# A ring of ten half-size units, one transfer for each piece, in a cached-attention decode step

## The chip, the cores and the metric

The kernel runs on one core of one Trainium2 chip. The metric is the device time of that core in microseconds (us), lower is better; a kernel's time is the median over its runs. The profile describes one execution, and its span runs from the first to the last instruction.

## What is computed

One decode step mixes an attention block over a long cache with a small gated MLP, for four sequences of one token each:

```python
x = A_x                                            # [4, 1, 1024], bf16
g = sigmoid((x * gate_w).sum(-1, keepdims=True))
# attention block: H = 32 heads of 128, Sk = 8192 cached keys
q = (x @ wq) split into heads
scores = einsum("bhqd,bhkd->bhqk", q, k_cache) * 128 ** -0.5
o = einsum("bhqk,bhkd->bhqd", softmax(scores), v_cache)
a = merge_heads(o) @ wo
# MLP block: with one token per sequence the routing always selects it
y = (silu(x @ w_gate) * (x @ w_up)) @ w_down * sigmoid(x @ w_r)
b = x + y
out = g * a + (1 - g) * b
```

`k_cache` and `v_cache` are [4, 32, 8192, 128] in bf16, 268 MB each. The weights together are some 39 MB. Each byte is read once.

## The kernel before, in words

**Pieces.** K and V are each read in ND = 32 pieces. A piece is four heads of one sequence: 128 partitions (four heads by 32 stretches of 256 keys), 64 KB on each, 8.4 MB in all. K piece d and V piece d belong to the same heads. Eight pieces make a group g (GD = 8), which has one softmax. A piece has RD = 4 quarters of 64 keys per partition, 16 KB each, numbered n.

**Order.** The program is one sequence, and PE, DVE and POOL run it in exactly that order. It starts with the query weights (wq), the gate weights, K0, K1 and the up weights; then K2 to K7; then K8, V0, K9, V1 and so on, V running eight pieces behind K. After K31 come the down weights (`wd_piece`) and V23 to V31. The output weights wo come last, in blocks of 1 MB and less. All loads are issued by SP in this order; a load waits on SP until the part of the ring that it overwrites has been read, and the loads after it wait behind it.

**The ring.** All of these loads land in one SBUF buffer of 160 KB per partition. Before, it has NS = 5 slots of 32 KB, half a piece each. `slots(2)` deals them out by turns, so successive pieces take slots 0-1, 2-3, 4-0, 1-2, 3-4 and again. A piece on two adjoining slots is one transfer; one on slots 4 and 0 is two transfers of 4 MB. Pieces V26 to V28 are always in two halves (`apart`), and V29 to V31 are cut further.

**A K piece** (`k_pair`). DVE transposes eight half-quarters (steps 0 to 7, two for each quarter) from the ring into one of three buffers TB (L494); for each step PE multiplies it with the spread query Z, eight matmuls into the scores S_ps (L499). So the ring is read by DVE alone here, and quarter n has been read when step 2n+1 is done. The quarters are used in the order 0 to 3.

**A V piece** (`v_pair`). PE alone reads the ring: 64 matmuls, 16 for each quarter, into the sums o_ps (L579), weighted by PB, the spread probabilities.

**Work hung onto the steps of K pieces.** After every second V piece the sums are emptied: ACT writes the first part (L605), and three DVE operations (L609, `sums`) add the others into OS. They are queued in `full` and flushed after step 2 of the next K piece. `finish`, eight small matmuls and in some pieces a sum more (L625), is flushed after step 4, and the scaling into OT (L637, `late`) after step 6. For the first group, softmax is put into the steps of K8: its `first` part after step 0 (maxima, then the exponential on ACT into a TB buffer, L530) and its `second` part after step 1 (transpose into PT, L535, then the spreading into PB on ACT and POOL). For the later groups both run right behind the last K piece of the group.

**The change of stage after K31.** The PSUM banks of the scores are given up (`scores.close()`) and taken over by the accumulator `acc` of the output. So `wd_piece`, whose matmuls (L287) write `acc`, comes on PE behind K31 and behind the exponential that reads the last scores. It reads the down weights row block by row block: 27 rows of 2 KB per partition with two matmuls each, then five shorter ones, in that order. V23 comes on PE behind it.

Of the kernel before, what the change touches and what calls it, by code (L numbers as in the profile page):

```python
# [8 lines left out]
BF = mybir.dt.bfloat16  # L9
# [103 lines left out]
def kernel(  # L113
# [15 lines left out]
    nc = tc.nc  # L129
    P = 128  # L130
# [20 lines left out]
    NB = 512  # L151
    NH = D // NB
    RING = JR * Dh
    NS = 5
    assert Sq == 1 and Dh == P and D % P == 0 and F % (P * FR) == 0
    assert H % GH == 0 and JR == 128 and RD * GD == QP and D % NB == 0
    scale = float(Dh) ** -0.5
# [11 lines left out]
    nc.at_finalize(drop_implied)  # L169
    nc.at_finalize(begin_early)  # L170

    ring = const.tile([P, NS, RING], BF, name="ring")
    turn = [0]


# [5 lines left out]
        tb_turn[0] += 1  # L181
        return t[0:rows, 0:n] if dtype == BF else t[0:rows, 0:2 * n].bitcast(dtype)

    def slots(n):
        at = turn[0]
        turn[0] = (at + n) % NS
        return at

    flat = ring[:].rearrange("p s n -> p (s n)")

    def load_pair(src, n, apart=False):

        a = slots(2)
        if a + 1 < NS and not apart:
            lo = a * RING
            nc.sync.dma_start(out=flat[:, lo:lo + 2 * n], in_=src)
            return [flat[:, lo:lo + n], flat[:, lo + n:lo + 2 * n]]
        halves = [ring[:, a], ring[:, (a + 1) % NS]]
        for i, half in enumerate(halves):
            nc.sync.dma_start(out=half[:, 0:n], in_=src[:, i * n:(i + 1) * n])  # L200
        return halves


    S0 = scp.tile([P, 4, NB], F32, name="S_ps")
# [8 lines left out]
        return b[:, 0:n].rearrange("p (%s) -> p %s" % (" ".join(names), " ".join(names)), **dict(zip(names, shape)))  # L213

    N = H * Dh
    wq_at = load_pair(A_wq.rearrange("(c t) n -> c (t n)", t=DT), DT // 2 * N)
    NX = Bn + 2
    x6 = const.tile([NX, D], BF)
    nc.sync.dma_start(out=x6[0:Bn], in_=x2)
# [134 lines left out]

    def gu_piece(view, w_i):

        ws = load_pair(view.rearrange("(c t) f -> c (t f)", t=DT), TW * F)

        def cols(w, t, i):
            row = w[:, t * F:t * F + FB].rearrange("p (f m) -> p f m", m=FI)  # L360
            if i < FG - 1:
                return [(0, FR, row[:, :, FR * i:FR * i + FR])]
            return [(0, FR - 1, row[:, :, FR * i:FI]), (FR - 1, FR, w[:, t * F + FB:(t + 1) * F])]
        x_rows(o_ps[w_i], ws, FG, cols)
# [28 lines left out]
        nc.vector.tensor_tensor(out=hS[:], in0=hs_ps[0:72], in1=cS[:], op=ALU.mult)  # L393

    def wd_piece():
        a = slots(2)
        assert a + 1 < NS and (FI + SX) * D == 2 * RING
        w = flat[:, a * RING:(a + 2) * RING]
        at = FI * D
        nc.sync.dma_start(out=w[:, 0:at], in_=wdv)  # L400
        for u in range(2):
            nc.sync.dma_start(out=w[32 * u:32 * u + 12, at:at + SX * D], in_=wd_apart[u])
        nc.sync.dma_start(out=w[64:72, at:at + D], in_=wd_rest)
        parts = [(hT[:, i // FR, i % FR, :], w[:, i * D:(i + 1) * D]) for i in range(FI)]
        parts += [(hS[:, v, :], w[0:72, at + v * D:at + (v + 1) * D]) for v in range(SX)]
        for i, (lhsT, rows) in enumerate(parts):
            for n in range(NH):
                mm_acc(n, lhsT, rows[:, n * NB:(n + 1) * NB], start=(i == 0))
# [11 lines left out]
                                 rhs=OT[:, WB * g0 + k:WB * g1:WB, :], start=True, stop=True, skip_group_check=True)  # L420
        nc.vector.tensor_copy(out=LT[:, :, g0:g1, :], in_=lp)  # L421

    wo_home = {}

    def wo_block(g, r0=0, r1=FR, half=None):

        home, at = divmod(g, 4)
        if home not in wo_home:
            wo_home[home] = ring[:, slots(1)].rearrange("p (g r n) -> p g r n", g=4, r=FR)
        w = wo_home[home][:, at]  # L430
        if half is None:
            nc.sync.dma_start(out=w[:, r0:r1].rearrange("p r n -> p (r n)"),
                              in_=wov[:, g, r0:r1].rearrange("p r n -> p (r n)"))
        else:
            nc.sync.dma_start(out=w[:, r0, half * NB:(half + 1) * NB], in_=wov[:, g, r0, half * NB:(half + 1) * NB])

        def use():
            for r in range(r0, r1):
                for n in range(NH) if half is None else [half]:
                    mm_acc(n, LT[:, r, g, :], w[:, r, n * NB:(n + 1) * NB])  # L440
        return use
# [25 lines left out]
    def kv_view(cache, d):  # L467
        b, h0 = heads(d)
        return cache[b, h0:h0 + NQ].rearrange("h (r j) d -> (h r) (j d)", j=2 * JR)
# [8 lines left out]
    def k_pair(d):  # L478
        g, t = divmod(d, GD)
        Z = Zt[d % 2]  # L480
        if d == 0:
            spread(0)
        if t == 0:
            S_ps[g] = S0
        sps = S_ps[g]
        ks = load_pair(kv_view(A_k_cache, d), RING)
        for n in range(RD):
            kn = ks[n // JT].rearrange("p (c j h m) -> p c h j m", c=JT, h=2, m=Dh // 2)[:, n % JT]
            s = QP - 1 - (RD * t + n)
            for half in range(2):  # L490
                step = 2 * n + half
                flat_t = turned(P, CJ * Dh // 2)
                T = flat_t.rearrange("p (j i e) -> p j i e", j=CJ, e=2)
                nc.vector.transpose(out=flat_t.bitcast(U32).rearrange("p (j i) -> p j i", j=CJ), in_=kn[:, half].bitcast(U32))  # L494
                if step < 2 and ahead:
                    ahead.pop(0)()
                for e in range(2):
                    for z in range(4):
                        nc.tensor.matmul(sps[:, z, :], lhsT=Z[:, 2 * half + e, s:s + P], rhs=T[:, 16 * z:16 * z + 16, :, e],  # L499
                                         start=(t + n + half + e == 0),  # L500
                                         stop=(t == GD - 1 and n == RD - 1 and half + e == 2))
                if step == 2:
                    flush_sums()
                if step == RD and d + 1 < ND:
                    spread(d + 1)
                if step == RD:
                    flush()
                if step == RD + 2:
                    flush_late()
        if t == GD - 1:  # L510
            ahead.extend(softmax(g))
            while g > 0 and ahead:
                ahead.pop(0)()

    def softmax(g):
        sps = S_ps.pop(g)
        PTs = turned(P, 4 * NB)

        def first():

            nc.vector.tensor_reduce(out=mx[:, 0:1], in_=sps[:].rearrange("p z n -> p (z n)"), axis=AX.X, op=ALU.max)  # L521
            nc.vector.transpose(out=mxT[:].bitcast(U32), in_=mx[:].bitcast(U32))
            gm = stat.tile([P, GD], F32, tag="gm")
            nc.vector.tensor_reduce(out=gm[:], in_=mxT[:].rearrange("p (t r) -> p t r", r=RD), axis=AX.X, op=ALU.max)
            nc.vector.tensor_scalar(out=ng[:].rearrange("p (t r) -> p t r", r=RD), in0=gm[:].unsqueeze(2).to_broadcast([P, GD, RD]),
                                    scalar1=-scale, scalar2=None, op0=ALU.mult)
            nc.vector.transpose(out=ngT[:].bitcast(U32), in_=ng[:].bitcast(U32))  # L527
            negm = ngT
            rs = stat.tile([P, 1], F32, tag="rs")
            nc.scalar.activation(out=PTs, in_=sps[:].rearrange("p z n -> p (z n)"), func=ACT.Exp, bias=negm[:, 0:1], scale=scale, accum_out=rs[:, 0:1])  # L530
            rs_t[g] = rs

        def second():
            PT = ptp.tile([P, CJ, 32], BF, name="PT", tag="PT")
            nc.vector.transpose(out=PT[:].rearrange("p j i -> p (j i)"), in_=PTs)  # L535
            PT_t[g] = PT
            if g == 0:
                spread_p(0, NW)
            elif g == NG - 1:
                spread_p(GD * g, NW - 1)  # L540

        return [first, second]
# [16 lines left out]
    def v_pair(d):  # L559
# [4 lines left out]
        flush_sums()  # L564
        vv = kv_view(A_v_cache, d)
        if d < ND - 3:
            vs = load_pair(vv, RING, apart=d >= ND - GD + 2)
        else:
            vs = [ring[:, slots(1)] for _ in range(2)]
            for half, cuts in ((0, 1), (1, 2)) if d < ND - 1 else ((0, 2), (1, 4)):  # L570
                for c in range(cuts):
                    lo, hi = c * RING // cuts, (c + 1) * RING // cuts
                    nc.sync.dma_start(out=vs[half][:, lo:hi], in_=vv[:, half * RING + lo:half * RING + hi])
        for u in range(4 * RD):
            n, z = divmod(u, 4)
            vn = vs[n // JT]
            for w in range(4):
                j0 = CJ * (n % JT) + 16 * z + 4 * w
                nc.tensor.matmul(o_ps[w // 2][row:row + NM, w % 2, :],  # L579
                                 lhsT=PB[:, RD * (d % NW) + n, z].rearrange("p w s j -> p (w s j)"),  # L580
                                 rhs=vn[:, j0 * Dh:(j0 + 4) * Dh], start=(u == 0), stop=(u == 4 * RD - 1),
                                 skip_group_check=True)
            if u == 1:
                flush()
            if u == 7:
                flush_late()
# [132 lines left out]
```

## Time and profile before

The runs took 1342.68 to 1342.78 us, median 1342.69.

| what | value |
|---|---|
| span of the profiled execution | 1340.5 us |
| PE, DVE, ACT, POOL busy | 1067.9, 638.3, 57.7, 66.6 us |
| bytes read | 575.68 MB, 429 GB/s over the span |
| granted TensorE clock, mean | 0.912 of full |
| one transpose of a K step (L494) | 2278 ns, 256 of them |
| one V sum on DVE (L609) | 737 ns, 33 of them |
| wq, the first transfer, issue to landing | 21.9 us |

The profile has the busy time of each engine, the span in 40 equal slices (a digit is the busy share in tenths), the chain of work that ended last, groups of equal instructions with what ended the idle time before them, and the transfers by source line. A timeline gives start, length and the releaser of single instructions. The trace also has each packet that a DMA engine moved, and for each transfer the times at which the 16 DMA engines reported their shares as landed; a transfer counts as landed with the last of the 16.

### The profile page before, as it was taken

Reading aid. Unit: us, or ns where it says so; the run is one execution under the profiler, and the core shown is the slowest. Engines: PE = TensorE matmul, PEld = TensorE weight load, DVE = VectorE, ACT = ScalarE, POOL = GpSimd, SP = SyncE. Lnnn points to the kernel's source line nnn. Section 1 sums busy time; section 2 is a strip of 40 time slices with the busy share of each in tenths; the row PEclk is TensorE's granted clock in tenths of the full one; section 3 lists DMA queues with packets and bytes.
Section 4 is the critical chain, followed back from the end, with each engine's and each line's share of the span. In section 5 each row is a group of like instructions: output and inputs, shape, how many; then the busy total and the mean of one; then the engine's idle time right before and its main releaser. Section 6 shows DMA issues by size and latency. Waiting matters only on the chain.

```text
span 1340.5 us, 6937 instructions
## 1 busy us (share of the span) xinstructions
PE 1067.9 (80%) x4654; PEld 141.3 (11%) x1422; DVE 638.3 (48%) x385; ACT 57.7 (4%) x58; POOL 66.6 (5%) x174
## 2 busy tenths in 40 slices
PE   2666878887778788777879778789697879889888
PEld 0101000001011010101001010101011011111111
DVE  2555988556544347554436256646145555100001
ACT  0000000100010000100010000100000000110000
POOL 2000000100010000100010000100001000100000
PEclk9787999898998998898989888899898889889889
DMA  9999999999999999999999999999999999999998
GB/s 415 433 436 435 437 436 424 438 430 430 435 437 426 439 431 428 433 438 431 434 433 433 436 433 438 419 434 431 438 433 441 426 423 435 438 425 430 429 425 348
DMA packets 15512, 576.14 MB, mean 430 GB/s; under 512 B 1740, under 2 KB 2004, under 8 KB 3170
## 3 DMA queue, kind: packets, MB, share of 16 engines
q1 hardware_dynamic: 15474, 575.69, 99.7%
q8 instruction: 24, 0.39, 0.1%
q14 instruction: 6, 0.05, 0.0%
q10 hardware_dynamic: 8, 0.00, 0.0%
HBM read 575.68 MB, written 0.01 MB: 429 GB/s over the span
## 4 chain that ended last, share of the span: by engine, by line
DMA 62%; DVE 22%; PE 13%; another core or an unknown queue 1%; issue 0%; ACT 0%; SPq 0%; DVEq 0%
DMA ring<-in_A_k_cache_dram 51%; DVE TB L494 20%; DMA ring<-in_A_v_cache_dram 9%; PE o_ps L579 8%; PE S_ps L499 2%; PE acc L287 2%; DVE OS L609 2%; DMA x<-in_gate_w_dram 2%; DVE mx L521 0%; PE o_ps L333 0%; PE S_ps L333 0%; PE led L625 0%; DVE PT L535 0%; ACT TB L530 0%
## 5 line engine op out<-in xcount | busy, mean ns | idle before, releaser
L494 DVE STREAM_TRANSPOSE TB<-ring 128x2048 uint32<-128x2048 uint32 x256 | 568.2, 2278 | 471.7 <-DMA ring<-in_A_k_cache_dram 463.9
L499 PE MATMUL S_ps<-TB,Z 128*128 128x512 bf16 x2048 | 531.5, 414 | 186.0 <-DVE TB L494 178.4
L579 PE MATMUL o_ps<-ring,PB 128*64 128x512 bf16 x2048 | 468.5, 392 | 44.9 <-DMA ring<-in_A_v_cache_dram 43.7
L499 PEld LDWEIGHTS <-Z 128*128 128x128 bf16 x512 | 53.0, 103 | 649.6 <-issue 649.6
L579 PEld LDWEIGHTS <-PB 128*64 128x64 bf16 x512 | 57.6, 112 | 447.8 <-issue 443.4
L617 DVE SCALAR_TENSOR_TENSOR OS<-o_ps,mE,OS 128x512 f32<-128x512 f32 x5 | 3.8, 751 | 134.9 <-ACT OS L615 134.9
L476 POOL COPY Z<-qa 32x4 bf16<-32x4 bf16 x128 | 25.6, 200 | 719.2 <-PE S_ps L499 693.2
L555 POOL COPY PB<-PT 32x1024 bf16<-32x1024 bf16 (+3 forms) x23 | 33.3, 1446 | 456.8 <-PE o_ps L579 350.7
L605 ACT ACTIVATE OS<-o_ps,mE 128x512 f32<-128x512 f32 x11 | 7.6, 687 | 673.6 <-PE o_ps L579 673.6
L553 ACT COPY PB<-PT 32x1024 bf16<-32x1024 bf16 (+3 forms) x21 | 30.3, 1443 | 22.3 <-PE o_ps L579 17.3
L609 DVE SCALAR_TENSOR_TENSOR OS<-o_ps,mE,OS 128x512 f32<-128x512 f32 x33 | 24.3, 737 | 1.5
L530 ACT ACTIVATE TB<-S_ps,mx 128x2048 bf16<-128x2048 f32 x4 | 7.9, 1967 | 321.9 <-DVE mx L527 321.9
L287 PE MATMUL acc<-ring,hT 128*4 128x512 bf16 x54 | 14.7, 444 | 5.4 <-ACT TB L530 5.4
L245 PE MATMUL S_ps<-identb,x 6*128 6x6 bf16 x8 | 0.6, 196 | 22.6 <-DMA x<-in_gate_w_dram 22.6
L333 PE MATMUL o_ps<-ring,xw 128*4 128x512 bf16 (+2 forms) x128 | 13.2, 499 | 4.8 <-DMA ring<-in_B_w_gate_dram 4.8
L287 PE MATMUL acc<-ring,LT 128*4 128x512 bf16 x64 | 14.7, 379 | 0.4 <-DVE LT L421 0.4
L625 PEld LDWEIGHTS o_ps<-selg,OS 128*128 128x128 f32 x88 | 11.5, 191 | 9.3 <-issue 8.8
L535 DVE STREAM_TRANSPOSE PT<-TB 128x2048 bf16<-128x2048 bf16 x4 | 9.2, 2312 | 6.4 <-ACT TB L530 6.4
L521 DVE TENSOR_REDUCE mx<-S_ps 128x1 f32<-128x2048 f32 x4 | 9.1, 2282 | 6.2 <-PE S_ps L499 6.2
L625 PE MATMUL o_ps<-selg,OS 128*128 128x8 f32 x88 | 10.5, 245 | 0.0
L637 DVE SCALAR_TENSOR_TENSOR OT<-led,sgb,rinv 128x8 bf16<-128x8 f32 x5 | 1.2, 237 | 18.2 <-PE led L625 18.2
L615 ACT ACTIVATE OS<-o_ps,mE 128x512 f32<-128x512 f32 x5 | 3.4, 687 | 147.9 <-PE o_ps L579 147.9
(83 smaller groups left out, 89.2 us busy)
## 6 DMA issues: line engine op xcount, KB each, us to landing
ring<-in_A_v_cache_dram SPq DMA_DIRECT2D x18, 4096.0 KB, 28.9
ring<-in_A_k_cache_dram SPq DMA_DIRECT2D x14, 4096.0 KB, 33.2
ring<-in_A_v_cache_dram SPq DMA_DIRECT2D x6, 2048.0 KB, 36.7
ring<-in_B_w_gate_dram SPq DMA_DIRECT2D x1, 7168.0 KB
ring<-in_B_w_up_dram SPq DMA_DIRECT2D x1, 7168.0 KB, 37.1
ring<-in_B_w_down_dram SPq DMA_DIRECT2D x1, 6912.0 KB
ring<-in_A_wo_dram SPq DMA_DIRECT2D x4, 1024.0 KB, 32.5
ring<-in_A_v_cache_dram SPq DMA_DIRECT2D x4, 1024.0 KB, 36.0
```

The source lines that it names most:

```text
L287: nc.tensor.matmul(acc(n), lhsT=lhsT, rhs=rhs, start=start, stop=True, skip_group_check=True)
L333: nc.tensor.matmul(ps[32 * k:32 * k + Bn, z, :].rearrange("p (f r) -> p f r", r=FR)[:, :, lo:hi], lhsT=xT[TW * half + t], rhs=rhs, start=( ...
L476: nc.gpsimd.tensor_copy(out=Z[at, :, QP - 1 + QP * q], in_=qa[at, :, h0 + q, b])
L494: nc.vector.transpose(out=flat_t.bitcast(U32).rearrange("p (j i) -> p j i", j=CJ), in_=kn[:, half].bitcast(U32))
L499: nc.tensor.matmul(sps[:, z, :], lhsT=Z[:, 2 * half + e, s:s + P], rhs=T[:, 16 * z:16 * z + 16, :, e], start=(t + n + half + e == 0), stop ...
L521: nc.vector.tensor_reduce(out=mx[:, 0:1], in_=sps[:].rearrange("p z n -> p (z n)"), axis=AX.X, op=ALU.max)
L535: nc.vector.transpose(out=PT[:].rearrange("p j i -> p (j i)"), in_=PTs)
L553: nc.scalar.copy(out=Bv[at, :, :, q, :], in_=Pv[at])
L555: nc.gpsimd.tensor_copy(out=Bv[at, :, :, q, :], in_=Pv[at])
L579: nc.tensor.matmul(o_ps[w // 2][row:row + NM, w % 2, :], lhsT=PB[:, RD * (d % NW) + n, z].rearrange("p w s j -> p (w s j)"), rhs=vn[:, j0 ...
L609: nc.vector.scalar_tensor_tensor(out=OS[:], in0=o_ps[w // 2][:, w % 2, :], scalar=mE[:, w:w + 1], in1=OS[:], op0=ALU.mult, op1=ALU.add)
L625: nc.tensor.matmul(oT, lhsT=OS[:, q * Dh:(q + 1) * Dh], rhs=selg[:, q].rearrange("p t s -> p (t s)"), start=(q == 0), stop=(q == 3), skip_ ...
```

## The change

The ring keeps its 160 KB and is now ten units of 16 KB, a quarter of a piece each (U = 8192 elements). A piece takes four adjoining units, always in one stretch. `place()` deals the stretches out by turns at the two ends of the ring, and gives the order in which the quarters are used:

| piece number k, mod 4 | units | order of use |
|---|---|---|
| 0 | 0 to 3 | down (3, 2, 1, 0) |
| 1 | 6 to 9 | up (6, 7, 8, 9) |
| 2 | 1 to 4 | up (1, 2, 3, 4) |
| 3 | 5 to 8 | down (8, 7, 6, 5) |

Successive pieces at one end share three units, and these three are the first three used of the older piece. Only the order of K and V quarters follows the table; wq, gate, up and down weights keep theirs. By the calls of `place()`, wq is piece 0, gate 1, K0 2, K1 3, up 4, K2 to K7 5 to 10, K8 11, V0 12, K9 13, V1 14, ..., K31 57, the down weights 58, V23 59, V24 60 and V31 67.

Every piece is one transfer but V26 to V31, which stay cut as they were; the halves of V26 to V28 are loaded in the order of use. The eight wo blocks go to units 0 to 3.

In a K piece the V sums are flushed after step 5 (the sixth), `finish` after step 6 and the scaling after step 7. The second part of the first softmax comes after step 5 in place of step 1, and its exponential is written into unit 4 of the ring in place of a TB buffer.

```diff
-    NS = 5
+    U = JR // 2 * Dh
+    NU = 10
...
-    ring = const.tile([P, NS, RING], BF, name="ring")
+    ring = const.tile([P, NU * U], BF, name="ring")
+    flat = ring[:]
...
+    def place():
+
+        k = turn[0]
+        turn[0] += 1
+        late = k // 2 % 2
+        first = (6 - late) if k % 2 else late
+        up = (k % 2 == 0) == (late == 1)
+        return first * U, list(range(4)) if up else list(range(3, -1, -1))
 
     def load_pair(src, n, apart=False):
 
-        a = slots(2)
-        if a + 1 < NS and not apart:
-            lo = a * RING
+        lo, order = place()
+        if not apart:
             nc.sync.dma_start(out=flat[:, lo:lo + 2 * n], in_=src)
-            return [flat[:, lo:lo + n], flat[:, lo + n:lo + 2 * n]]
-        halves = [ring[:, a], ring[:, (a + 1) % NS]]
-        for i, half in enumerate(halves):
-            nc.sync.dma_start(out=half[:, 0:n], in_=src[:, i * n:(i + 1) * n])
-        return halves
+        else:
+            for i in (0, 1) if order[0] == 0 else (1, 0):
+                nc.sync.dma_start(out=flat[:, lo + i * n:lo + (i + 1) * n], in_=src[:, i * n:(i + 1) * n])
+        return [flat[:, lo:lo + n], flat[:, lo + n:lo + 2 * n]], order
...
     def wd_piece():
-        a = slots(2)
-        assert a + 1 < NS and (FI + SX) * D == 2 * RING
-        w = flat[:, a * RING:(a + 2) * RING]
+        lo, _ = place()
+        assert (FI + SX) * D == 4 * U
+        w = flat[:, lo:lo + 4 * U]
...
-        home, at = divmod(g, 4)
-        if home not in wo_home:
-            wo_home[home] = ring[:, slots(1)].rearrange("p (g r n) -> p g r n", g=4, r=FR)
-        w = wo_home[home][:, at]
+        w = flat[:, g * FR * D:(g + 1) * FR * D].rearrange("p (r n) -> p r n", r=FR)
...
-        for n in range(RD):
+        for at, n in enumerate(order):
...
-                step = 2 * n + half
+                step = 2 * at + half
...
-                if step < 2 and ahead:
+                if step in (0, 2 * RD - 3) and ahead:
                     ahead.pop(0)()
...
-                if step == 2:
+                if step == 2 * RD - 3:
                     flush_sums()
                 if step == RD and d + 1 < ND:
                     spread(d + 1)
-                if step == RD:
+                if step == 2 * RD - 2:
                     flush()
-                if step == RD + 2:
+                if step == 2 * RD - 1:
                     flush_late()
...
-        PTs = turned(P, 4 * NB)
+        PTs = turned(P, 4 * NB) if g else flat[:, 4 * U:4 * U + 4 * NB]
...
         if d < ND - 3:
-            vs = load_pair(vv, RING, apart=d >= ND - GD + 2)
+            vs, order = load_pair(vv, RING, apart=d >= ND - GD + 2)
         else:
-            vs = [ring[:, slots(1)] for _ in range(2)]
+            at, _ = place()
+            order = list(range(RD))
+            vs = [flat[:, at + i * RING:at + (i + 1) * RING] for i in range(2)]
...
-            n, z = divmod(u, 4)
+            n, z = order[u // 4], u % 4
```

More of the change, by code (lines that the diff above doesn't have):

```diff
@@ L182, in turned @@
         return t[0:rows, 0:n] if dtype == BF else t[0:rows, 0:2 * n].bitcast(dtype)
[L184 to L189, printed above, removed]
+    def place():
[5 more added lines that the diff above has]
+        return first * U, list(range(4)) if up else list(range(3, -1, -1))
     def load_pair(src, n, apart=False):
-        a = slots(2)
-        if a + 1 < NS and not apart:
-            lo = a * RING
+        lo, order = place()
+        if not apart:
             nc.sync.dma_start(out=flat[:, lo:lo + 2 * n], in_=src)
-            return [flat[:, lo:lo + n], flat[:, lo + n:lo + 2 * n]]
-        halves = [ring[:, a], ring[:, (a + 1) % NS]]
-        for i, half in enumerate(halves):
-            nc.sync.dma_start(out=half[:, 0:n], in_=src[:, i * n:(i + 1) * n])
-        return halves
+        else:
+            for i in (0, 1) if order[0] == 0 else (1, 0):
+                nc.sync.dma_start(out=flat[:, lo + i * n:lo + (i + 1) * n], in_=src[:, i * n:(i + 1) * n])
+        return [flat[:, lo:lo + n], flat[:, lo + n:lo + 2 * n]], order
     S0 = scp.tile([P, 4, NB], F32, name="S_ps")
@@ L215 @@
     N = H * Dh
-    wq_at = load_pair(A_wq.rearrange("(c t) n -> c (t n)", t=DT), DT // 2 * N)
+    wq_at, _ = load_pair(A_wq.rearrange("(c t) n -> c (t n)", t=DT), DT // 2 * N)
     NX = Bn + 2
@@ L355, in gu_piece @@
     def gu_piece(view, w_i):
-        ws = load_pair(view.rearrange("(c t) f -> c (t f)", t=DT), TW * F)
+        ws, _ = load_pair(view.rearrange("(c t) f -> c (t f)", t=DT), TW * F)
         def cols(w, t, i):
@@ L421, in o_rows @@
         nc.vector.tensor_copy(out=LT[:, :, g0:g1, :], in_=lp)
-    wo_home = {}
     def wo_block(g, r0=0, r1=FR, half=None):
-        home, at = divmod(g, 4)
-        if home not in wo_home:
-            wo_home[home] = ring[:, slots(1)].rearrange("p (g r n) -> p g r n", g=4, r=FR)
-        w = wo_home[home][:, at]
+        w = flat[:, g * FR * D:(g + 1) * FR * D].rearrange("p (r n) -> p r n", r=FR)
         if half is None:
@@ L485, in k_pair @@
         sps = S_ps[g]
-        ks = load_pair(kv_view(A_k_cache, d), RING)
-        for n in range(RD):
+        ks, order = load_pair(kv_view(A_k_cache, d), RING)
+        for at, n in enumerate(order):
             kn = ks[n // JT].rearrange("p (c j h m) -> p c h j m", c=JT, h=2, m=Dh // 2)[:, n % JT]
@@ L499, in k_pair @@
                         nc.tensor.matmul(sps[:, z, :], lhsT=Z[:, 2 * half + e, s:s + P], rhs=T[:, 16 * z:16 * z + 16, :, e],
-                                         start=(t + n + half + e == 0),
-                                         stop=(t == GD - 1 and n == RD - 1 and half + e == 2))
-                if step == 2:
+                                         start=(t + at + half + e == 0),
+                                         stop=(t == GD - 1 and at == RD - 1 and half + e == 2))
+                if step == 2 * RD - 3:
                     flush_sums()
```

## The prediction

> **What bounds the kernel.** I read the page's 40 slices and its transfers first, then the landing times of the transfers, then timelines at the places where a new wait could bite.
>
> ```profile
> DMA  9999999999999999999999999999999999999998
> GB/s 415 433 436 435 437 436 424 438 430 430 435 437 426 439 431 428 433 438 431 434 433 433 436 433 438 419 434 431 438 433 441 426 423 435 438 425 430 429 425 348
> ...
> q8 instruction: 24, 0.39, 0.1%
> ```
>
> The DMA engines are never idle, and no slice moves more than 441 GB/s. A whole piece lands every 19.35 us (8.4 MB). The packets say the same: one of 64 KB takes 2418 ns at best, each of the 16 engines carries 8 of them for a piece, and 8 x 2.418 = 19.34. So the time is that of the bytes, plus start and tail. PE (80%) and DVE (48%) only matter through what they release: a change can gain what transfers cost above this pace, and lose wherever the queue runs empty.
>
> **Part 1, one transfer instead of two.** The page's transfers by line (count, KB each, median us from issue to landing) have 14 K and 18 V transfers of 4 MB.
>
> ```profile
> ring<-in_A_v_cache_dram SPq DMA_DIRECT2D x18, 4096.0 KB, 28.9
> ring<-in_A_k_cache_dram SPq DMA_DIRECT2D x14, 4096.0 KB, 33.2
> ...
> ring<-in_A_wq_dram SPq DMA_DIRECT2D x1, 21.9
> ```
>
> Eight stay (six halves of V26 to V28, one each of V29 and V30), so 24 become 12. Two halves land 9.71 us apart each, 19.42 a piece, against 19.35 for a whole: 12 x 0.07 = **-0.84 us**. The 32 KB packets agree: 1213 ns against half of 2418. The Trainium skill's page "DMA: Bandwidth & Descriptors" (Anatomy of one DMA) fits each transfer at 2.0 us plus its bytes over 436 GB/s; by it 12 transfers fewer would be 24 us, an estimate. The landings 0.07 us over show that here the next transfer covers the fixed part, so the row decides.
>
> **Part 2, later releases.** Before, a one-transfer piece goes out when half of the piece two earlier is read; now when three quarters are. What must hold is seen at wq, the only transfer issued into an empty queue: issue to landing 21.9, which is 19.35 + **2.55 us**. So a load must be issued 2.55 us before its predecessor lands, and every us less is a us lost. wq's first packets end at 4.2, seven more bring the last to 21.15, and landings are reported from 21.4: 0.25 of it is the report, and wq pays a first use. So the true figure lies between about 1.5 (first packets start 1.0 after issue, and take 0.7 longer than the others) and 2.55; I use 2.55.
>
> - K pieces: before, the half release is 8.90 us after landing (four transposes at 2.21, chain of waits at 270.23). Now six: 13.3. The following V lands at 19.35, so 6.0 us remain, 3.4 to spare. Moving the sums (2.35 us) behind step 5 keeps them out of this; their cost is hidden by the 19 us in which DVE waits for the next K. If that cover were gone, 11 such sets x 2.35 = 26 us would count.
> - V pieces: with sums, V starts about 22.5 us after K lands (308.9 to 331.43); three quarters of its 13.93 are read 10.5 us later, at 33.0. The next K lands at 38.7: 5.7 remain. `finish` and the scaling stand behind one step's matmuls less than before; I add 0.3 to V's start, hidden in the same 5.7.
> - Start: K0 waits for all of wq (28.7), gate lands at 39; K0 is used from 59.4, not 49.7, and DVE is done at 77.1 before K1 lands at 78.8. K2 goes out at 92.2, up lands at 95.7: 3.5 remain. Nothing is lost.
> - Tail: wo and V31 wait for quarters of V28 to V30 that are read over 10 us earlier. Nothing.
>
> **Part 3, K8 with the first softmax.** The timeline of DVE at K8 (start, length, engine, line, operation, count, and what ended the idle time before):
>
> ```profile
> 231.44 2.31 DVE L494 STREAM_TRANSPOSE TB<-ring 128x2048 uint32<-128x2048 uint32 x1 [1.69 <-DMA ring<-in_A_k_cache_dram]
> 233.68 2.25 DVE L521 TENSOR_REDUCE mx<-S_ps 128x1 f32<-128x2048 f32 x1
> ...
> 236.78 2.27 DVE L494 STREAM_TRANSPOSE TB<-ring 128x2048 uint32<-128x2048 uint32 x1
> 238.98 2.31 DVE L535 STREAM_TRANSPOSE PT<-TB 128x2048 bf16<-128x2048 bf16 x1
> 241.33 13.28 DVE L494 STREAM_TRANSPOSE TB<-ring 128x2048 uint32<-128x2048 uint32 x6
> ```
>
> Without the second part, steps 1 and 2 end at 241.26. Step 3 needs a TB back from step 0, whose matmuls start at 239.00 behind the exponential and, at the low clock there (32 in 8.85 us, where V's 64 take 13.93), end near 242.2: 0.9 us lost. Step 5 ends near 248.9, and K9 goes out. It lands at 248.9 + 21.9 = 270.8, before at 270.1: **+0.7** (0 to 1.5). V1 then goes out near 268.2, just in time. The second part's later end (251.2, spread by 255.2) is hidden by K8's matmuls, which end near 257.6.
>
> **Part 4, the down weights.** This is the step that I think decides. The timeline behind K31, all engines, and below it SP's:
>
> ```profile
> 1115.70 6.70 DVE L494 STREAM_TRANSPOSE TB<-ring 128x2048 uint32<-128x2048 uint32 x3 [9.02 <-DMA ring<-in_A_k_cache_dram]
> ...
> 1136.42 1.96 PE L499 MATMUL S_ps<-TB,Z 128*128 128x512 bf16 x8 [0.23 <-DVE TB L494]
> ...
> 1143.78 14.74 PE L287 MATMUL acc<-ring,hT 128*4 128x512 bf16 x54 [5.40 <-ACT TB L530]
> ...
> 1156.42 0.09 PEld L287 LDWEIGHTS <-hT 128*4 128x4 bf16 x1 [0.35 <-issue]
> ...
> 1180.72 3.44 PE L579 MATMUL o_ps<-ring,PB 128*64 128x512 bf16 x8 [2.61 <-DMA ring<-in_A_v_cache_dram]
> ```
>
> ```profile
> 1153.81 0.33 SPq L196 DMA_DIRECT2D ring<-in_A_v_cache_dram  x1
> ```
>
> Before, K31 is a split piece: its first half lands at 1115.6 and DVE starts on it 9.7 us ahead of the second (1125.3). The matmuls of the down weights start at 1143.78, released by the exponential; V24 needs the first 16 rows of them and goes out at 1153.81, 7.4 us before V23 lands at 1161.24 (V24 is waited for until 1180.7, one piece later).
>
> Now K31 is one transfer: DVE starts at 1125.4, eight transposes take 17.66 (as K2's row has them), PE's last step 2.0, and maxima and exponential 5.36 (1138.42 to 1143.78): `acc` starts at 1150.4. V23 goes out when six transposes are done, 1138.7, and the down weights land near 1141.8: 3.1 remain, enough. V24 lies on units 0 to 3, the down weights on 1 to 4, so it waits for 24 rows: the load for the 24th is at 1156.42, its two matmuls are done by 1157.3, 13.5 after the start. V24 goes out at 1163.9, **2.7 us after V23 has landed**, and lands at 1163.9 + 21.9 = 1185.8 against 1180.6: **+5.2** (by 1.5 for the restart it is 4.2). By the skill's 2.0 us for the fixed part (same page and section) it would be 2.7 + 2.0 = 4.7, an estimate. Behind V24 on SP stand V25 and all later loads, and PE only follows them: nothing after it has slack to give back, so it all reaches the end. V25 then goes out at 1181.4 (three quarters of V23, on PE from 1169.1), 4.4 before V24 lands: in time.
>
> **Part 5, the lead of single engines.** The page's 24 instruction fetches delay one DMA engine each, by some 0.96 us in the packets. The first and last of the 16 land 1.64 us apart at 49.7, 3.15 at 542.7, 4.66 at 989.7; a fetch on an engine that is ahead costs nothing. An empty queue lets the leaders idle and lines all up, and the next fetch is paid in full. After V24 this is one fetch, +1.0; after K9 +0.96 near 265, but the two jumps of 1.4 before (542, 989) come later or smaller. Sum: **+0.4** (-0.6 to +2).
>
> **Sum.** -0.84 + 0.7 + 5.2 + 0.4 = +5.5, with 2.55 for the restart the upper side; with 2.2 it is +4.9. I take +5.3: the span goes from 1340.5 to 1345.8. The median of the runs is 2.2 above the span, outside it and untouched: **1348.0 us**.
>
> **Rivals.** (a) **V24 is in time.** It decides from the point at which V24 goes out by 1158.7, 5.2 us earlier than I work out. For it: if the clock is not halved at the start of `acc` (weight loads 0.85 us apart for seven rows, later 0.43), 24 rows take 10.4 us instead of 13.5, and a restart price of 1.5 takes 1 more; the rest would need the wait to cover less than I think. Against: PE idles 5.4 us ahead of `acc` before and after alike. If it holds, and K9 too, the time is 1342.69 - 0.84 = 1341.9.
>
> (b) **The queue starves in every pair.** If the 6.0 and 5.7 us are eaten by the leaders (4.7) and the restart (2.55), each fetch after the start counts in full: some 22 x 0.96 = 21, less the 3 paid before, on top of +5: up to 1366, some 1355 if half of it. Before speaks against it: K9 went out at 245.86, 4.8 us before V0 landed at 250.67, and landed 19.44 us after it. And eight engines alone share the fetches in turn, so the leaders that idle are mostly those that are never hit.
>
> (c) **Faster.** Over 0.2% is 2.7 us; the bytes at 19.35 a piece leave 0.84. It would take a price of transfers that no row shows.
>
> **How the numbers follow.** My forecast 0.68, from 1345.4 to 1351 (restart 1.5 to 2.55, K9 0 to 1.5, lead -0.6 to +2); (a) 0.19, between 1341.5 and 1344.5; (b) 0.11; (c) 0.02. The range from 1341.5 to 1351 leaves out (b) and (c). A measurement of this kernel can tell 0.2%, 2.7 us, from no change: slower is the forecast and (b), 0.78 with what of the forecast falls below 1345.4 taken off and part of (a) added; same 0.20; faster 0.02.
>
> **What would show it.** Landings 19.35 apart with no 9.71 pairs until V26; K9's load issued near 249; `acc` starting near 1150 with the scores' exponential ahead of it; V24's load issued near 1164, an idle gap of 4 to 5 us in the DMA share there and nowhere else; V24 landing near 1186; landing spread under 1 us right after. I am wrong if V24 goes out before V23 lands, or if gaps stand at other pieces.

## The result, and the profile after

The changed kernel is slower: 1353.64 us median over six runs (1347.81 to 1354.85), beside 1342.94 for the kernel before on the same chip. The ratio is 1.007, 95% interval 1.006 to 1.0081. The direction was forecast, the size was not: 1348.0 was predicted, at most 1351. New is also the scatter: the runs of the kernel before lie within 1.5 us, these within 7. The profiled execution is one of the shorter: 1350.36 us, its span 1348.6.

Page of the kernel after (span, DMA busy share and rate in 40 slices, transfers by line):

```profile
span 1348.6 us, 6898 instructions
...
DMA  9999999999999999999999999999999999999998
GB/s 416 454 410 432 436 435 432 407 433 430 414 436 435 434 432 430 434 432 434 433 434 434 435 432 402 436 435 432 435 434 434 433 434 430 391 419 434 423 428 351
...
ring<-in_A_v_cache_dram SPq DMA_DIRECT2D x8, 4096.0 KB, 17.2
...
ring<-in_A_k_cache_dram SPq DMA_DIRECT2D x32, 25.3
```

The 4 MB transfers of K are gone: 32 transfers for 32 pieces, and the landings stand 19.35 us apart where nothing else happens. The median from issue to landing is 25.3, so 6.0 us remain between an issue and the landing of the piece before it. I call that the **lead** of a load. The slices stay at 9, but the rate now dips to 407, 402 and 391. The eighth slice holds K9, the 25th V15, the 35th V24.

The landing times show where the 8.1 us of this execution arose. All are in us from the start of the span; "later" is against the kernel before. An instruction fetch (part 5 of the prediction) "counts" when the engine that it delays is the last to land, so that the landing of the whole transfer moves.

```
landing of   before    after   later   what happened since the row above
K1            78.77    78.89    0.1
K8           231.34   232.21    0.9    two fetches counted (K2 went out with a lead of 3.5)
K9           270.14   273.75    3.6    queue ran empty, and the fetch at 267.0 counted
K20          697.68   699.98    2.3    before paid a fetch at K15; merged transfers
K21          736.46   739.98    3.5    a fetch counted
V16          871.99   876.82    4.8    a fetch counted, after V15 went out with a lead of 2.6
K31         1125.31  1128.59    3.3    before paid a fetch at V19
V23         1161.24  1166.21    5.0    a step at the down weights
V24         1180.59  1187.28    6.7    queue ran empty
V25         1199.95  1208.03    8.1    a fetch counted
```

At K8 the release comes late, as the timeline shows (start, length, engine, line, operation, count, releaser of the idle time):

```profile
232.30 2.31 DVE L491 STREAM_TRANSPOSE TB<-ring 128x2048 uint32<-128x2048 uint32 x1 [1.69 <-DMA ring<-in_A_k_cache_dram]
...
243.47 2.31 DVE L491 STREAM_TRANSPOSE TB<-ring 128x2048 uint32<-128x2048 uint32 x1 [1.37 <-PE S_ps L496]
246.05 4.50 DVE L491 STREAM_TRANSPOSE TB<-ring 128x2048 uint32<-128x2048 uint32 x2 [0.27 <-PE S_ps L496]
250.48 2.27 DVE L532 STREAM_TRANSPOSE PT<-ring 128x2048 bf16<-128x2048 bf16 x1
...
250.58 0.33 SPq L199 DMA_DIRECT2D ring<-in_A_k_cache_dram  x1
...
1128.61 17.66 DVE L491 STREAM_TRANSPOSE TB<-ring 128x2048 uint32<-128x2048 uint32 x8 [17.67 <-DMA ring<-in_A_k_cache_dram]
...
1153.69 13.10 PE L289 MATMUL acc<-ring,hT 128*4 128x512 bf16 x54 [5.40 <-ACT TB L527]
...
1165.52 0.33 SPq L199 DMA_DIRECT2D ring<-in_A_v_cache_dram  x1
```

The sixth transpose of K8 ends at 250.5, and K9's load goes out at 250.58, 1.0 us before V0 has landed. Behind K31 the eight transposes run in one stretch, `acc` starts 25.1 us after K31's landing, and V24's load goes out at 1165.52, 0.7 us before V23 has landed.

### The profile page after: what moved, and what is told of

Same layout as the page of the kernel before. It is cut to its first block, busy times and chain, and to the rows that moved or that the text cites. A ratio compares the mean times of both kernels' runs of the same rounds, so it can differ in the third digit from the quotient of the medians.

```text
span 1348.6 us, 6898 instructions
## 1 busy us (share of the span) xinstructions
PE 1064.1 (79%) x4654; PEld 141.9 (11%) x1422; DVE 639.4 (47%) x385; ACT 57.6 (4%) x58; POOL 66.8 (5%) x174
## 4 chain that ended last, share of the span: by engine, by line
DMA 62%; DVE 27%; PE 10%; ACT 0%; issue 0%; SPq 0%; DVEq 0%
DMA ring<-in_A_k_cache_dram 53%; DVE TB L491 26%; DMA ring<-in_A_v_cache_dram 6%; PE o_ps L578 5%; DMA ring<-in_B_w_gate_dram 3%; PE acc L289 2%; PE S_ps L496 2%; PE o_ps L335 0%; DVE mx L518 0%; PE led L624 0%; ACT TB L527 0%; ACT ring L527 0%; DVE OS L616 0%; ACT OS L614 0%; DVE TB L616 0%
## 5 line engine op out<-in xcount | busy, mean ns | idle before, releaser
L496 PE MATMUL S_ps<-TB,Z 128*128 128x512 bf16 x2048 | 540.7, 421 | 223.1 <-DVE TB L491 215.4
L578 PE MATMUL o_ps<-ring,PB 128*64 128x512 bf16 x2048 | 456.6, 385 | 20.2 <-DMA ring<-in_A_v_cache_dram 19.0
```

The lines of the kernel that those rows point to most:

```text
L578: nc.tensor.matmul(o_ps[w // 2][row:row + NM, w % 2, :], lhsT=PB[:, RD * (d % NW) + n, z].rearrange("p w s j -> p (w s j)"), rhs=vn[:, j0 ...
```

## The experiments

Every kernel here computes the whole step. Times are medians. The kernel before, run beside each of the three sets (e, f and g), lay at 1342.7 to 1342.8.

| kernel | median | lowest to highest | ratio to before, 95% interval |
|---|---|---|---|
| e1_again: the changed kernel | 1352.19 | 1349.23 to 1353.25 | 1.0066 (1.0054 to 1.0078) |
| e2_k31_halves | 1350.76 | 1345.73 to 1352.25 | 1.0050 (1.0035 to 1.0064) |
| e3_sums_third | 1356.46 | 1355.85 to 1356.93 | 1.0101 (1.0086 to 1.0116) |
| e4_k9_halves | 1351.98 | 1350.22 to 1356.21 | 1.0071 (1.0059 to 1.0083) |
| f1_sums_alone | 1342.86 | 1342.38 to 1343.43 | 1.0000 (0.9991 to 1.0008) |
| f2_quarter_all | 1348.40 | 1348.06 to 1349.79 | 1.0041 (1.0028 to 1.0054) |
| f3_sums_spread | 1349.35 | 1348.34 to 1350.18 | 1.0048 (1.0034 to 1.0061) |
| f4_fixes | 1346.12 | 1345.28 to 1347.78 | 1.0024 (1.0014 to 1.0033) |
| g2_spread_k31 | 1344.74 | 1343.73 to 1346.42 | 1.0014 (1.0005 to 1.0023) |
| g1_fixes_k31 | 1342.91 | 1342.53 to 1344.08 | 1.0000 (0.9992 to 1.0009) |

**e1_again**, no edit.

> The changed kernel once more, for its spread and a second trace. Theory A (two fixed places, K9 and V24, let the queue run empty, and the lost lead of the DMA engines makes later instruction fetches count): times between 1347 and 1355 again, and in the trace the added us stand at K9 (+2 to +3.5), at V24 with the piece after it (+3 to +7), and in single jumps of 1 to 1.5 us. Theory B (the V sums, now behind the sixth step, leave PE idle just ahead of a V piece, its clock is halved there in some executions, and that V's successor is issued too late): V pieces behind sums show leads under 4 us in different places from execution to execution, 2 to 5 of 11, and these make most of the spread of the times.

The profiled execution (1353.25) has the gaps in the same two places: K9 2.2 us, V24 2.3 with 1.1 more at V25. The rest lies elsewhere than in the first trace: 1.4 at K17, 0.7 at K20, 2.1 at V21. Both theories have their part. The V pieces behind sums are V2, V4 and so on to V20; each releases the load of the next V piece. The leads of those ten loads, V3 to V21:

```
kernel             leads of V3, V5, ... V21 (us)                     under 5
after              4.0  5.6  5.9  5.8  5.5  7.1  2.6  7.2  5.6  5.8     2
e1_again           5.6  5.8  5.8  7.3  2.3  3.2  6.5  5.8  5.6  2.9     3
e2_k31_halves      4.3  5.7  5.8  5.8  5.7  3.6  6.0  5.9  4.2  5.7     3
e4_k9_halves       3.8  5.8  2.9  3.3  4.0  5.7  5.8  6.8  5.5  5.7     4
f3_sums_spread     5.9  6.3  6.6  6.4  5.5  7.4  6.5  6.4  5.6  6.3     0
```

Most stand at the forecast 5.7; some fall to 2 to 4, in other places each time. In the four traces that have the pause (all but f3), 12 of the 40 leads are under 5. Ahead of each of the 12 the clock records have a stretch of 3.4 or 6.8 us at half clock, and ahead of none of the other 28. The timeline of PE at one of them (after, ahead of V14, whose successor V15 had 2.6) shows why, and the windows below it (last columns: granted clock, DMA share, GB/s):

```profile
796.53 2.36 PE L496 MATMUL S_ps<-TB,Z 128*128 128x512 bf16 x8 [2.46 <-DVE TB L491]
798.69 1.71 PE L624 MATMUL o_ps<-selg,OS 128*128 128x8 f32 x8
800.25 3.58 PE L496 MATMUL S_ps<-TB,Z 128*128 128x512 bf16 x8
803.76 14.47 PE L578 MATMUL o_ps<-ring,PB 128*64 128x512 bf16 x64
```

```profile
793.00:798.00 5.00, 2.54 (x12) 0.19 (x2) 4.96 (x4) 0.00 (x0) 0.00 (x0) 0.99 1.00 433
798.00:803.00 5.00, 5.00 (x18) 2.12 (x10) 0.91 (x2) 0.00 (x0) 0.00 (x0) 0.50 1.00 433
```

While DVE makes the three sums in one go, PE waits 2.46 us for the next transpose. Then the granted clock is 0.50 from 797.9 on for 6.8 us: `finish` takes 1.71 us where it took 0.95, the eight matmuls of the last step 3.58 where 1.96 is usual, and V14 starts late and slow. In e1_again such a half-speed stretch starts at 641.4, ahead of the lead of 2.3, and at 719.9, ahead of the 3.2.

**f3_sums_spread** takes that pause away; `finish` comes one step later in it as well.

```diff
-                if step == 2 * RD - 3:
-                    flush_sums()
+                if step >= 2 * RD - 3 and full:
+                    full.pop(0)()
...
-                if step == 2 * RD - 2:
+                if step == 2 * RD - 1:
                     flush()
```

`sum_up` queues the three sums singly.

> The changed kernel; the three sums come one each after the sixth, seventh and eighth step, finish and scaling after the eighth. Theory B: PE has no idle stretch of 2.4 us ahead of V any more, no V piece behind sums has a lead under 5 us, and the median falls by 2 to 4 us. Theory C without B: leads under 5 stay at some V pieces, less than 1.5 us faster.

1349.35: 2.8 us under e1_again, the scatter down from 4.0 to 1.8, no lead of V3 to V21 under 5.5. Timeline of PE at the same piece:

```profile
794.11 1.96 PE L496 MATMUL S_ps<-TB,Z 128*128 128x512 bf16 x8 [0.89 <-DVE TB L491]
796.97 1.96 PE L496 MATMUL S_ps<-TB,Z 128*128 128x512 bf16 x8 [0.89 <-DVE TB L491]
798.77 0.95 PE L623 MATMUL o_ps<-selg,OS 128*128 128x8 f32 x8
799.65 14.00 PE L578 MATMUL o_ps<-ring,PB 128*64 128x512 bf16 x64
```

```profile
796.00:801.00 5.00, 4.11 (x24) 1.36 (x11) 1.78 (x3) 0.00 (x0) 0.78 (x4) 1.00 1.06 459
```

Two waits of 0.89 in place of one of 2.46, every step at 1.96, the clock at 1.00, and V14 starts 2.5 us after its own landing where it was 5.7 (798.04 to 803.76). The kernels differ only in where the sums and `finish` stand. Where the clock isn't halved, the changed kernel starts these V pieces 1.6 to 3.3 us after their landing, mostly 3.0, so the other place of `finish` and of the sums by itself is worth some 0.5 us; the short leads come from the pause and the half clock behind it.

**e3_sums_third** puts sums, `finish` and the scaling back to where they were before, in the changed ring.

```diff
-                if step == 2 * RD - 3:
+                if step == 2:
                     flush_sums()
...
-                if step == 2 * RD - 2:
+                if step == RD:
                     flush()
...
-                if step == 2 * RD - 1:
+                if step == RD + 2:
                     flush_late()
```

> The sums, finish and the scaling go back to the third, fifth and seventh step; everything else as changed. Theory B: no V piece behind sums has a lead under 5 us, the spread over executions falls under 3 us, and the median falls by 2 to 5 us. Theory A: the K pieces with sums are released 2.35 us later (lead 3.6 in place of 5.9), which costs nothing or up to 2 us, and the spread stays.

1356.46, the slowest of all, with a scatter of 1.1 us. The V leads are as theory B had them (5.5 to 7.3), but the loads of K11, K13 and so on now have 3.7, and that was not free, as I had thought it might be. Beside the gaps at K9 and V24 the time goes in single steps of 0.4 to 1.3 us at K11, K14, K17, V10, K23 and K29. Each of these landings comes 12 to 22 us after an instruction fetch of 16 KB, which delays one DMA engine, so it is that of the transfer that the fetch falls into or of the next. The spread of the 16 engines (how far apart the first and the last land), which a lead of 3.7 cuts, is mostly 1.2 to 2.9 us there, and few engines are far enough ahead to take a fetch unseen.

**f1_sums_alone** is the other half: the kernel before, with only the later place of the sums, `finish` and the scaling.

> The kernel before with only the later place of sums, finish and scaling. Theory C (the loss comes from releases that are late, so that single DMA engines run dry and instruction fetches on them count): leads of V pieces stay over 6 us here, so nothing: 1342.7 within 1. Theory B (the later sums cost by themselves, through PE's clock ahead of V): 1344 or more.

1342.86, no difference. The V loads there have leads of 6.0 and more, the spread of the engines grows to 5.1 us, and only two steps over 0.2 us remain that the kernel before hasn't. The half clock is there all the same, at four of the ten V pieces behind sums; behind V2 the next load's lead falls to 6.0, and nothing is lost. So neither the pause nor the clock costs by itself; they cost through a short lead.

**f2_quarter_all** gives every load back its lead, without touching layout or order.

```diff
+        if quarter:
+            a, b = ((3 * U, 4 * U), (0, 3 * U)) if order[0] == 0 else ((0, U), (U, 4 * U))
+            for x, y in (a, b):
+                nc.sync.dma_start(out=flat[:, lo + x:lo + y], in_=src[:, x:y])
-        if not apart:
+        elif not apart:
```

> The changed kernel; K2 to K31 and V0 to V25 are each loaded in two transfers, first the 16 KB unit that is free early, then the other three. Theory C: every lead rises by 4.8 us, no landing is over 19.5 us after the one before but for the fetches that the kernel before pays too, the spread of the 16 engines grows to 3 us and more again; 56 transfers more at 0.07 us are 3.9: 1344 to 1347, with a spread of executions under 2 us. Rival (the layout with its down orders, or the single transfers themselves, cost): no faster than the changed kernel, 1351 to 1356.

1348.40, 3.8 us faster than the changed kernel though it has 56 transfers more, and 1.4 over the range that I gave. The leads are 10.9 at the K pieces. The spread of the engines grows in the trace from 1.9 at K9 to 4.8 at K31, as before the change, and the only steps are the two that the kernel before has as well (by K15 and V19). At K31 the trace stands 3.2 us behind the kernel before, which is what the added transfers cost; 2.4 more come behind K31, where `acc` starts as late as in the changed kernel; 1.3 of them are one step at V28, behind a spread of 1.7. The down orders and the places in the ring, which f2 keeps, are thereby not the cause of the steps up to K31.

**e4_k9_halves** loads K9 in two halves, first the units that are free or freed first.

> K9 alone is loaded as two halves, first the half that lies on the units that are free or freed first. Theory A: the gap of 2.8 us at K9 goes, and what the lost lead costs after it: 2.5 to 4 us faster than the changed kernel. Theory B: 2.5 to 3 us at most, and the spread stays as it is.

1351.98: no gain over e1_again. The gap at K9 is gone (0.03 us), but V1, which waits for V0's matmuls behind the first softmax, then goes out with a lead of 1.7 and lands 0.9 late with all engines in line; 1.3 follows at K11, and this execution has four short V leads. I had priced K9 alone and not the next wait behind it.

**e2_k31_halves** and **g2_spread_k31** load K31 in two halves, as the kernel before did, in the changed kernel and in f3_sums_spread.

```diff
-        ks, order = load_pair(kv_view(A_k_cache, d), RING)
+        ks, order = load_pair(kv_view(A_k_cache, d), RING, apart=d == ND - 1)
```

> K31 alone is loaded as two halves. Theory A: DVE starts K31 9.7 us earlier, acc starts some 8 us earlier, V24 is issued 6 us or more ahead of V23's landing, and the stretch from K31's landing to V24's is 55.3 us again, not 58.7: 3 to 6 us faster than the changed kernel. Theory B: the places of the loss are elsewhere, less than 1.5 us faster.

> The changed kernel with the sums spread over three steps, and K31 in two halves; K9 as changed. The gap at V24 with the fetch behind it is 3 to 4.5 us in the traces: 1345 to 1346.5, against 1349.4 with the sums spread alone. If K31's single landing isn't what makes V24 late: 1348 or more.

e2: 1350.76, 1.4 under e1_again, but with a scatter of 6.5 us that hides the answer; its trace, of the shortest execution, has V24's load 7.1 us ahead and no gap. On the calmer base the answer is plain: 1344.74 against 1349.35, **4.6 us**. In g2's timeline `acc` starts 17.5 us after K31's landing (1126.36) in place of 25.1:

```profile
1143.83 14.29 PE L289 MATMUL acc<-ring,hT 128*4 128x512 bf16 x54 [5.40 <-ACT TB L527]
```

**f4_fixes** is f3_sums_spread with K2, K9, V1 and V24 in two transfers, the free unit first; **g1_fixes_k31** adds V25 to these and loads K31 in halves.

> Sums spread as in f3_sums_spread, and K2, K9, V1 and V24 alone loaded in two transfers, the free unit first. Theory C with B: all gaps go (K9, V24), 4 transfers more cost 0.3, some fetches are still paid: 1342.5 to 1346. If the cause is in the layout or the down orders: over 1349.

> f4_fixes with K31 in two halves and V25 in two transfers as well. If what f4_fixes still loses (2.1 us at V25, 1.4 at the down weights, in its trace) comes from the late start of acc and the small leads behind it: V25's jump goes, 1343 to 1344.5. If the losses lie elsewhere: 1345.5 or more, as f4_fixes.

f4: 1346.12. Up to K31 its trace is 0.5 us ahead of the kernel before; then it loses 1.4 at the down weights and 2.1 at V25, where `acc` is late as ever and the lead is 4.0. g1: 1342.91, the time of the kernel before. Its trace is 0.5 us ahead at K29, and 1.7 go at the down weights again. Why a step remains there isn't settled: their two small transfers put 80 KB more on three of the 16 engines, but no run moved them. The drift of the engines seems to bear on it: from K31 to V23 f2, with the same transfers and the engines 4.8 us apart at K31, takes 0.2 us longer than the kernel before, and the other nine traces of the changed ring, at 1.8 to 3.4, take 0.5 to 2.2 longer. No version here beats the kernel before.

Added up by medians: 1352.19, less 2.8 for the pause of the sums, less 4.6 for K31 in one landing, less 1.8 for the loads of K2, K9, V1, V24 and V25, is 1342.9. The sum goes by this order of the runs (f3, g2, g1); in another the parts differ: with K31 still in one landing, K2, K9, V1 and V24 in two transfers each took 3.2 together off f3. The median of the changed kernel's first six runs lies 1.5 above e1's.

## Why the prediction was wrong, and where it was right

**Right.** The bound (the landings 19.35 us apart), the worth of the merged transfers (under 1 us in all), the lead of the K loads (6.0 forecast, mostly 5.9 to 6.0 measured) and the two places where the queue runs empty. Of V24's chain `acc` came 25.1 us after K31's landing, the very figure, and issue to landing took 21.76, forecast 21.9. From K31 to V25 the two traces after took 79.4 and 80.2 us against 74.6: 4.8 and 5.6, where 5.2 and one fetch of 1.0 were forecast; removed on a calm base, the step is worth 4.6. Rival (a) is out, and so is rival (c). Two figures of the prediction are slightly off and change nothing: V0 of the kernel before landed at 250.77, not 250.67, and with 2.2 for the restart at K9 and V24 the sum is +4.8, not +4.9. The skill's fit of 2.0 us for each transfer, which parts 1 and 4 set beside the rows, stands on the named page for transfers that GpSimd issues; those here are issued by SP.

**Right in the sum, in part by luck: V24.** Its load went out 0.7 us (0.2 in e1) before V23 had landed, where 2.7 us after was forecast; the prediction had named this as a sign of being wrong, as it had gaps at other pieces. The gap at V24 was 1.7 and 2.3 us in place of 5.2. One reason is that the 24 rows took 11.8 us (12.9 in e1) in place of 13.5: `acc` ran at half clock for 2.6 us (4.7), before for 6.0. The other is that V23 landed 1.7 and 2.2 us later behind K31 than before, at the step at the down weights. The sum had no term for that step ("3.1 remain, enough"), and it made up for what the gap lacked.

**Wrong: what the sums cost.** The step that failed is in part 2: "their cost is hidden by the 19 us in which DVE waits for the next K", and, of `finish` and the scaling, "I add 0.3 to V's start, hidden in the same 5.7". DVE does have the time. But a pause of 2.35 us on DVE is one of up to 2.46 on PE, just ahead of `finish` and V, and at some pieces PE's clock is halved for 3.4 or 6.8 us behind it. V's release then comes 1.7 to 3.4 us later, and the 5.7 that I counted on aren't there. This term, put at 0.3 and hidden, is worth 2.8 us and most of the scatter (e1 against f3). I had weighed the sums by what DVE loses and never asked what PE does meanwhile; before the change the same pause stood five steps ahead of V, on work with time to spare, and now it is two:

```profile
1097.83 5.37 PE L499 MATMUL S_ps<-TB,Z 128*128 128x512 bf16 x16 [2.02 <-DVE TB L494]
1103.04 0.95 PE L625 MATMUL o_ps<-selg,OS 128*128 128x8 f32 x8
1103.85 5.56 PE L499 MATMUL S_ps<-TB,Z 128*128 128x512 bf16 x24
```

The Trainium skill's page "TensorE: Matmul & The Clock Gate" (Part 1) halves the clock after an idle window of some 3.4 us. The traces agree on such a window: all changes of the clock in one trace lie on one grid of 3.41 us. But the window needn't be idle throughout: the clock was halved behind pauses of 1.97 to 2.46 us. Which pauses are hit is set by where they fall on that grid (last section).

**Mis-sized: the lead of single engines** (+0.4 forecast, "come later or smaller"). Rival (b), that short leads make the fetches count, was right in kind: e3 is it in the K loads, with 2.3 us less lead; it is 7.1 us slower than f3, which has no pause either, and 4.3 slower than e1. I gave it to all pairs or none. It acts at leads of 3.7 us and less: the spread sinks to 0.5 to 2.9 us, which fits engines that are ahead and run dry. The next fetch on the engine that is then last counts, 0.4 to 1.4 us each. The price of a fetch was low as well: one that counts in full costs 1.2 to 1.5 us and not 0.96 (K15 and V19 before 1.19 and 1.46; K21, V16 and V25 after 1.29, 1.38 and 1.40). In the packets the engine stands still for about 1 us, and its next packet of 64 KB takes 0.5 us longer than the 2.42 of the others.

**Mis-sized: K9** (+0.7 forecast, 2.2 to 2.8 in the traces). K8 itself landed up to 0.9 later, since K2's lead of 3.5 had already cost the engines their lead ("Nothing is lost" was wrong by that much; with K2 in two transfers, in f4, K8 is 0.1 late). The wait for a TB took 1.6 us in place of 0.9. Issue to landing took 23.2 in place of 21.9, but 15 of the 16 engines had landed after 21.75; the last came 1.4 later, by the fetch at 267.0, for which part 5 had added 0.96.

## What to carry to other kernels

Where the transfers set the time, the figure to watch is the lead: how long before the landing of its predecessor a load goes out. Here 6 us were enough, the room above that took up the pause and the half clock without loss (f1), and at 3.7 and less the fetches that followed mostly reached the end; saving 0.07 us for each transfer isn't worth giving up 4 us of lead. When work is moved off one engine's release, ask what the others do while it runs in its new place, above all what comes right behind it.

## What the runs showed of the hardware

- A load issued less than 1 us before or after the queue's last landing takes 21.8 to 22.0 us for 8.4 MB, against 19.35 in the stream (V24 of the changed kernel, of e1 and of f3: 21.76, 21.83, 22.00). K9's 23.16 holds a fetch of 1.4. V15, with a lead of 2.59, landed in time (21.94).
- The 16 DMA engines don't stay in step. Instruction fetches of 16 KB delay one of them at a time, by 1.2 to 1.5 us; with leads that are mostly 8 us and more (before, f1, f2) the first and last drift 4.7 to 5.1 us apart by K31, and that drift is a reserve. With leads of 6 and none much shorter (f4) it is 2.7 to 4.3 in the second half, with every other K lead at 3.7 (e3) mostly 1.2 to 2.9.
- The granted clock changes only on a grid of 3.41 us, which lies elsewhere in each execution (2.61 us after the start of the span in the trace after, 3.12 in e1, 2.41 in f3). In the six traces with the pause of the sums ahead of V (after, e1, e2, e4, f1, f2) there are 60 such pauses of 1.81 to 2.46 us. Half clock followed the 20 that put 1.97 to 2.46 us of idle time into one stretch of the grid, and none of the 40 that put 1.23 to 1.97 into one. Two waits of 0.89 us put at most 1.52 into one, and it followed none of them (40 places in f3, f4, g1 and g2).
